# Sparse attention and a softplus feed-forward on one core: weight conversion begun later and its steps queued behind the attention's

## The chip, the cores and the metric

The kernel runs on one core of a Trainium2 chip. The metric is device time in microseconds (us); lower is better. The kernel before took 1484.01 us (median of three runs, 1479.19 to 1485.22).

The core's engines work from queues of their own, each in order: TensorE (PE; its weight loads are PEld) multiplies and transposes, VectorE (DVE) and ScalarE (ACT) work on tiles and read TensorE's results from PSUM, GpSimd (POOL) works on tiles in SBUF, and SyncE (SP) issues all transfers here.

## The reference

For each of 8 x 8 heads with 576 rows of 64, attention in which only scores within tau of the row's maximum count, then a feed-forward on the 4608 rows of 512:

```python
scores = scale * np.matmul(q, k.transpose(0, 1, 3, 2))
thresh = np.max(scores, axis=-1, keepdims=True) - tau
scores = np.where(scores >= thresh, scores, -1000000000.0)
attn = np.exp(scores - max); attn = attn / (sum(attn) + 1e-09)
x = (attn @ v), heads side by side                  # 4608 x 512
h = x @ w_in                                        # 512 x 2048
g = np.maximum(h, 0.0) + np.log1p(np.exp(-np.abs(h)))
out = g @ w_out                                     # 2048 x 512
```

q, k and v are float32, the two weight matrices are 64-bit floats.

## The kernel before, in words

**Attention.** A unit is a pair of heads of one batch: 32 units, each with nine tiles of 128 rows, so 288 tiles. TensorE works in a reduced float format, so every operand is split into a high part and a low part and each product is made from two or three. For a tile, `scores` (L375) puts 128 x 576 scores into one of two PSUM buffers of two banks, `row_max` (L395) reduces them on VectorE, `exps` (L405) writes the exponentials on ScalarE, `mask` (L409) zeroes on VectorE what lies below the threshold and adds up the row. Then `weights_T` (L428) transposes the masked tile on TensorE, `weights_hi` (L468, ScalarE) and `weights_lo` (L483) make the two parts, and for each of four groups of columns in a unit `values` (L509) multiplies with v into a PSUM bank. The two halves of that result are added by `values_out` (L522): ScalarE copies one half to SBUF (through `copy`, L462), VectorE adds the other. In the first 36 tiles (TG) the low parts are made by TensorE and ScalarE (L492, L494, L464), later by VectorE (L125).

**Feed-forward.** From tile 41 on, `hidden` (L597, L610 to L614), `softplus` (L625) and `project` (L659, L668 to L672) work through chunks of 512 rows, spread between the steps of the attention so that TensorE has work while a tile waits for the other engines.

**PSUM.** Four banks (tag "g", GB = 4) serve the transposes of q and k, the hidden units, the outputs, the sums of the values and the row scales; four more hold the scores.

**Weights.** Both matrices come in 32 blocks of 128 x 512 64-bit floats. `to_f32` (L134) loads one (L168, 512 KB) and turns the bit patterns into float32: ScalarE takes the absolute value of the high words (L176), GpSimd clamps (L177), VectorE shifts left (L181), puts in the sign (L182) and three bits of the low words (L184). `parts` then splits the result on GpSimd (L118, L125). A block of w_in goes back to DRAM in that form (L208), and its pieces of memory are free again; a block of w_out stays. There are NFC = 16 pieces (`free`, `held`): a block in conversion takes two where it can, and a w_out block keeps a further one. With too few pieces (`took` below 2) the block uses other buffers and all its steps are emitted at once behind the load (`later_` then calls at once); with none at all, `force` first carries out deferred work early until some come free.

**Order.** The program is emitted tile by tile along a string of letters, PAT0 for the first 36 tiles and PAT after that:

```python
PAT = "ThRlefmpfxSwp"
PAT0 = "RMTeShlfpfxwp"
```

R, e, m, S are the reduction, exponential and mask of the next tile and the scores of the one after it, M, T, h, l the mask, transposes and parts of the present one, f a piece of feed-forward, x the unit's extras (among them `values`), w the next weight block if its time has come (one every second tile, from tile 1 to tile 63). Each p is a *point*, two in a tile: `defer(n, f)` (L754) emits f at the n-th point from now. So WD = 2 defers the first step of a block by one tile behind its load. The order of emission is a priority and not yet the order in the queues: the framework works out, when the program is built, when each instruction would be ready, and puts into each engine's queue the first that is ready. An instruction that is emitted later can so be queued ahead of one whose inputs come later in that calculation. On the chip the queue is then kept in order. `tc.add_manual_dep(..., NoSync, ...)` forces an order of two instructions of one queue without a semaphore.

Of the kernel before, what the change touches and what calls it, by code (L numbers as in the profile page):

```python
# [9 lines left out]
F32 = mybir.dt.float32  # L10
F32R = mybir.dt.float32r
U32 = mybir.dt.uint32
AF = mybir.ActivationFunctionType
ALU = mybir.AluOpType
# [18 lines left out]
LAG0 = 5  # L33
PAT = "ThRlefmpfxSwp"
PAT0 = "RMTeShlfpfxwp"
WD = 2
ST = (1, 3, 4, 4, 5, 6, 6, 8)
VO = (1, 1, 1, 0)
RT = 1
# [19 lines left out]
def tile_kernel(ctx: ExitStack, tc: tile.TileContext, q, k, v, tau, w_in, w_out, out):  # L59
# [8 lines left out]
    nc = tc.nc  # L68
# [5 lines left out]
    HS = S // 2  # L74
# [3 lines left out]
    NFC = DFF // P  # L78
# [28 lines left out]
                            op0=ALU.is_ge, op1=ALU.mult)  # L107
# [8 lines left out]
    def hi_of(eng, out_, in_):  # L116
        if eng is nc.gpsimd:
            eng.tensor_scalar(out=out_, in0=in_, scalar1=1.0, scalar2=1.0, op0=ALU.mult, op1=ALU.mult)  # L118
        elif eng is nc.scalar:
            eng.copy(out_, in_)  # L120
        else:
            eng.tensor_copy(out_, in_)  # L122

    def lo_of(eng, out_, in_, hi):
        eng.tensor_tensor(out=out_, in0=in_, in1=hi.bitcast(F32), op=ALU.subtract)  # L125
# [2 lines left out]

    free, held = [NFC], [0]

    def piece(dt, name):
        return cpool.tile([P, 2, DM], dt, tag="wo", bufs=NFC, name=name)

    def to_f32(src, want, name, then):  # L134

        keep = 1 if want else 0
        while free[0] < 1 + keep and free[0] < NFC - held[0]:
            force()  # L140
        took = max(0, min(2, free[0] - keep))
        if took:
            words = piece(F32R, f"wc_{name}")
        else:
            words = wpool.tile([P, 2, DM], F32R, tag="wi", bufs=WB, name=f"wc_{name}")
        if took > 1:
            m = piece(F32, f"wa_{name}")[:, 0, :]
        else:
            m = fpool.tile([P, 512], F32, tag="st", bufs=NST, name=f"ws_{name}")
        free[0] -= took + keep  # L150
        held[0] += keep

        later_ = defer if took > 1 else lambda n, f: f()
        w = piece(F32R, f"wo_{name}") if want else words

        def done():
            free[0] += took

        def parts():
            hi_of(nc.gpsimd, w[:, 0, :], m)  # L160
            lo_of(nc.gpsimd, w[:, 1, :], m, w[:, 0, :])

        if src.dtype == F32:
            nc.sync.dma_start(m, src)
            later_(WD, lambda: then(parts, w, done))
            return
        words = words.bitcast(U32).rearrange("p a n -> p (a n)")
        nc.sync.dma_start(words, src.bitcast(U32))  # L168
        words = words.rearrange("p (n t) -> p n t", t=2)
        low, high = words[:, :, 0], words[:, :, 1]  # L170
        mu = m.bitcast(U32)

        def first():
            nc.scalar.activation(m, high.bitcast(F32), AF.Abs, scale=2.0 ** 16)  # L176
            nc.gpsimd.tensor_scalar(out=m, in0=m, scalar1=W_MAX, scalar2=W_MIN, op0=ALU.min, op1=ALU.max)  # L177
            later_(1, second)

        def second():  # L180
            nc.vector.tensor_scalar(out=mu, in0=mu, scalar1=3, scalar2=None, op0=ALU.logical_shift_left)  # L181
            nc.vector.scalar_tensor_tensor(out=mu, in0=high, scalar=0x80000000, in1=mu,  # L182
                                           op0=ALU.bitwise_and, op1=ALU.bitwise_or)
            nc.vector.scalar_tensor_tensor(out=mu, in0=low, scalar=29, in1=mu,  # L184
                                           op0=ALU.logical_shift_right, op1=ALU.bitwise_or)
            later_(1, lambda: then(parts, w, done))

        later_(WD, first)

    ready = set()  # L190
# [25 lines left out]
    def prep_w_out(fc):  # L216
        def split(parts, w, free):
            wo[fc] = w
            parts()
            free()  # L220
            ready.add(("o", fc))

        to_f32(w_out[fc * P:(fc + 1) * P, :], True, f"o{fc}", split)
# [25 lines left out]
    for b in range(B):  # L249
        for kind in (("one", "two") if b < NSPLIT else ("all",)):  # L250
            for hp in range(NPAIR):
                s = Unit()
# [118 lines left out]
    e_all = cpool.tile([P, 2, S], F32, name="e_all")  # L371
# [31 lines left out]
        s.m[t] = (negm, thr)  # L403

    def exps(s, t):  # L405
        nc.scalar.activation(e_all[:, s.half[t], :].rearrange("p (h n) -> p h n", h=2), s.sp[t][:, :, 0:HS],  # L406
                             AF.Exp, bias=s.m[t][0], scale=1.0)

    def mask(s, t):  # L409
        e2 = e_all[:, s.half[t], :].rearrange("p (h n) -> p h n", h=2)  # L410
        nc.vector.scalar_tensor_tensor(out=e2, in0=s.sp[t][:, :, 0:HS], scalar=s.m.pop(t)[1], in1=e2,  # L411
                                       op0=ALU.is_ge, op1=ALU.mult, accum_out=s.sums[:, s.tiles.index(t):s.tiles.index(t) + 1])

    def group(s, g):
        if g not in s.grp:
# [45 lines left out]

    def copy(s, out_, in_):  # L462
        if s.neg:
            nc.scalar.activation(out_, in_, AF.Copy, scale=-1.0)  # L464
        else:
            nc.scalar.copy(out_, in_)  # L466

    def weights_hi(s, t):  # L468
        main, rest = s.sp[t]
        for g, c0, s0, n in s.place[t]:  # L470
            copy(s, group(s, g)[0][:, 0:NC, c0:c0 + n], main[:, :, s0:s0 + n])
        both = rests(s, t)
        if len(both) == 2:

            (g, c0, _, n), = s.place[both[0][0]]
            copy(s, group(s, g)[0][:, NC, c0:c0 + 2 * n].rearrange("p (k n) -> p k n", k=2),
                 rest.unsqueeze(1).to_broadcast([P, 2, n]))
            return
        for x, rows, up, _ in both:
            for g, c0, s0, n in s.place[x]:  # L480
                copy(s, group(s, g)[0][up, NC, c0:c0 + n], rest[rows, s0:s0 + n])
# [27 lines left out]
    def values(s, g):  # L509
        if g == 0:  # L510
            s.xp = apool.tile([P, S], F32, tag="xp", name=f"xp_{s.i}")
        j, x0, n, _ = s.groups[g]
        h, l = s.grp[g]
        vt = s.vt[j]
        o = ps_g.tile([P, 512], F32, tag="g", name=f"pv_{s.i}_{g}")
        for c in range(NC):
            nc.tensor.matmul(o[:, 0:n], vt[:, c, :], h[:, c, 0:n], start=(c == 0), stop=False)  # L517
            nc.tensor.matmul(o[:, 0:n], vt[:, c, :], l[:, c, 0:n], start=False, stop=False)  # L518
        nc.tensor.matmul(o[:, 0:n], vt[:, NC, :], h[:, NC, 0:n], start=False, stop=True)
        defer(1, lambda: values_out(s, g, o))  # L520

    def values_out(s, g, o):  # L522
        j, x0, n, _ = s.groups[g]
        keep = slice(j * D, (j + 1) * D)
        move = slice((1 - j) * D, (2 - j) * D)
        xs = s.xp[keep, x0:x0 + n]
        copy(s, xs, o[move, 0:n])
        if s.neg:
            nc.vector.tensor_tensor(out=xs, in0=xs, in1=o[keep, 0:n], op=ALU.subtract)
        else:  # L530
            nc.vector.tensor_tensor(out=xs, in0=o[keep, 0:n], in1=xs, op=ALU.add)

    def row_scales(s):
        nt = len(s.tiles)
# [219 lines left out]
    def defer(n, f):  # L754
        if n == 0:
            f()
        else:
            later.append((now["p"] + n, f))
# [8 lines left out]
    def force():  # L767
        _, f = later.pop(0)
        f()
# [6 lines left out]
    while sum(u.T for u in chunks) < NT:  # L776
# [4 lines left out]
        b, o = divmod(u.t0 + u.T - 1, S)  # L781
# [20 lines left out]
    for kind, g in WL:  # L802
        for m in range(4):
            n = len(prep)
# [75 lines left out]
    scores(*tiles[0])  # L880
    row_max(*tiles[0])
    exps(*tiles[0])
    scores(*tiles[1])
    for j in range(2):
# [3 lines left out]
    done = 0.0  # L888
    for g, (cur, t) in enumerate(tiles):
# [5 lines left out]
        for step in PAT0 + ("m" if g == TG - 1 else "") if g < TG else PAT:  # L895
            if step == "T":
                weights_T(cur, t)
            elif step == "h":
                weights_hi(cur, t)
            elif step == "l":  # L900
                weights_lo(cur, t)
            elif step == "R" and nxt:
                row_max(*nxt)
            elif step == "e" and nxt:
                exps(*nxt)
            elif step == "m" and nxt:
                mask(*nxt)
            elif step == "M":
                mask(cur, t)
            elif step == "f":  # L910
                upto += quota / PAT.count("f")
                while done < upto:
                    done += next(ffn)
            elif step == "x":
                extras(cur.i, cur.tiles.index(t))
            elif step == "S" and g + 2 < NS:
                scores(*tiles[g + 2])
            elif step == "w":
                while prep and prep[0][0] <= g:
                    _, f, a = prep.pop(0)  # L920
                    f(*a)
            elif step == "p":
                point()
# [38 lines left out]
```

## Time and profile before

| | |
|---|---|
| median of three runs | 1484.01 us |
| profiled execution | 1484.28 us, span 1482.5 us, mean granted TensorE clock 0.984 |
| busy: TensorE, its weight loads | 1411.4 us (95%), 1198.7 us (81%) |
| busy: VectorE, ScalarE, GpSimd | 1008.7 us (68%), 873.1 us (59%), 600.4 us (40%) |
| moved by DMA | 189.95 MB |
| mask L411 | 288 times, 815 ns each |
| exponential L406 | 288 times, 750 ns each |
| copy and addition of a sum (L466, L531; 400 to 1200 us) | 81 times, 418 and 472 ns (medians) |

Times are counted from the first instruction. A row of a timeline has the start, the length, the engine, the line and the tiles it writes and reads (out<-in); in brackets stands how long the engine was idle before it, and what ended that. A row of waits has who waited for whom, the total in us, how often, and the longest. Matmuls overlap, so a busy TensorE isn't TensorE at its peak; the granted clock (PEclk, 1.00 or 9 is full) says at what speed it ran. The first step on the first weight block stands at 12.8 us and the last load of one at 287.8 us, so the conversion lies in the first 300 us.

### The profile page before, as it was taken

Reading aid. Unit: us, or ns where it says so; the run is one execution under the profiler, and the core shown is the slowest. Engines: PE = TensorE matmul, PEld = TensorE weight load, DVE = VectorE, ACT = ScalarE, POOL = GpSimd, SP = SyncE. Lnnn points to the kernel's source line nnn. Section 1 sums busy time; section 2 is a strip of 40 time slices with the busy share of each in tenths; the row PEclk is TensorE's granted clock in tenths of the full one; section 3 lists DMA queues with packets and bytes.
Section 4 is the critical chain, followed back from the end, with each engine's and each line's share of the span. In section 5 each row is a group of like instructions: output and inputs, shape, how many; then the busy total and the mean of one; then the engine's idle time right before and its main releaser. Section 6 shows DMA issues by size and latency. Waiting matters only on the chain.

```text
span 1482.5 us, 23938 instructions
## 1 busy us (share of the span) xinstructions
PE 1411.4 (95%) x8024; PEld 1198.7 (81%) x8024; DVE 1008.7 (68%) x2251; ACT 873.1 (59%) x1671; POOL 600.4 (40%) x629
## 2 busy tenths in 40 slices
PE   5887889999999999999999999999999999999998
PEld 4777668788888888888888888888888888788887
DVE  6878778777777777777777777777777777411111
ACT  5777677565766576666666676657665666411110
POOL 4657565534433443344333443334334331323221
PEclk9999899999999999999999999999999999999999
DMA  6756575434443454335334544345333532343321
GB/s 183 199 151 193 151 215 173 130 104 134 129 120 116 119 157 115 98 102 151 110 105 113 149 118 119 108 134 152 114 113 100 153 99 81 103 142 120 120 88 43
DMA packets 131210, 189.95 MB, mean 128 GB/s; under 512 B 35312, under 2 KB 86800, under 8 KB 131088
## 3 DMA queue, kind: packets, MB, share of 16 engines
q1 hardware_dynamic: 131088, 188.43, 44.4%
q8 instruction: 64, 1.05, 0.3%
q14 instruction: 58, 0.48, 0.1%
HBM read 140.51 MB, written 27.41 MB: 113 GB/s over the span
## 4 chain that ended last, share of the span: by engine, by line
PE 76%; DVE 7%; ACT 5%; DMA 4%; issue 3%; POOL 3%; SPq 1%; POOLq 0%; ACTq 0%; DVEq 0%
PE s L392 10%; PE h L612 8%; PE h L610 8%; PE h L614 8%; PE o L672 7%; PE o L670 7%; PE o L668 7%; PE s L444 7%; PE pv L518 4%; PE pv L517 4%; DMA wc_i<-in_moe_w_in_dram 2%; PE tr L333 2%; DVE e_all L411 1%; DVE negm L398 1%; POOL g L125 1%
## 5 line engine op out<-in xcount | busy, mean ns | idle before, releaser
L466 ACT CAST gH<-s 128x512 fp32r<-128x512 f32 (+1 forms) x448 | 186.7, 466 | 150.7 <-PE s L444 145.9
L125 POOL TENSOR_TENSOR g<-st,g 128x512 fp32r<-128x512 f32 x144 | 191.8, 1350 | 193.6 <-DVE g L122 184.2
L411 DVE SCALAR_TENSOR_TENSOR e_all<-s,thr,e_all 128x576 f32<-128x576 f32 x288 | 234.4, 815 | 38.0 <-ACT e_all L406 34.6
L398 DVE TENSOR_REDUCE negm<-s 128x1 f32<-128x576 f32 x288 | 217.2, 755 | 48.5 <-PE s L392 40.8
L672 PE MATMUL o<-wo_o,g 128*128 128x512 f32 x576 | 232.8, 404 | 5.3 <-POOL g L125 5.3
L668 PE MATMUL o<-wo_o,g 128*128 128x512 f32 x576 | 233.5, 405 | 0.5 <-ACT g L120 0.4
L612 PE MATMUL h<-xl,wi 128*128 128x512 f32 x576 | 233.1, 405 | 0.0
L610 PE MATMUL h<-xh,wi 128*128 128x512 f32 x576 | 230.5, 400 | 0.4 <-ACT kT L337 0.4
L614 PE MATMUL h<-xh,wi 128*128 128x512 f32 x576 | 230.4, 400 | 0.0
L670 PE MATMUL o<-wo_o,g 128*128 128x512 f32 x576 | 229.9, 399 | 0.0
L406 ACT ACTIVATE e_all<-s,negm 128x576 f32<-128x576 f32 x288 | 216.0, 750 | 12.4 <-DVE negm L398 6.9
L125 DVE TENSOR_TENSOR gL<-s,gH 128x512 fp32r<-128x512 f32 (+1 forms) x280 | 175.0, 634 | 48.1 <-ACT gH L466 44.2
L392 PE MATMUL s<-kT,qT 128*128 128x288 f32 x1024 | 194.2, 312 | 7.4 <-DVE gH L125 4.4
L392 PEld LDWEIGHTS s<-kT,qT 128*128 128x128 f32 x1024 | 151.1, 193 | 25.1 <-issue 14.3
L444 PE MATMUL s<-identr,e_all 128*128 128x128 f32 x1008 | 155.2, 277 | 4.8 <-DVE e_all L411 4.7
L122 DVE CAST g<-st 128x512 fp32r<-128x512 f32 x128 | 57.8, 489 | 149.8 <-ACT st L632 149.3
L518 PE MATMUL pv<-gL,vt 128*128 128x320 f32 (+1 forms) x512 | 145.4, 304 | 5.0 <-DVE gL L125 4.8
L632 ACT ACTIVATE st<-h 128x512 f32<-128x512 f32 x144 | 78.3, 596 | 117.7 <-PE h L614 117.1
L517 PE MATMUL pv<-gH,vt 128*128 128x320 f32 (+1 forms) x512 | 145.6, 303 | 1.3 <-ACT gH L466 1.3
L672 PEld LDWEIGHTS o<-wo_o,g 128*128 128x128 f32 x576 | 109.2, 190 | 29.5 <-POOL g L125 10.9
L444 PEld LDWEIGHTS s<-identr,e_all 128*128 128x128 f32 x1008 | 116.0, 141 | 21.0 <-DVE e_all L411 12.8
L610 PEld LDWEIGHTS h<-xh,wi 128*128 128x128 f32 x576 | 108.9, 189 | 23.1 <-ACT kT L337 0.7
(105 smaller groups left out, 2381.2 us busy)
## 6 DMA issues: line engine op xcount, KB each, us to landing
wi<-wi_d SPq DMA_DIRECT2D x144, 512.0 KB
qT<-qT SPq DMA_DIRECT2D x124, 128.0 KB
R<-r_d SPq DMA_DIRECT2D x64, 144.0 KB
kn<-in_k_dram SPq DMA_DIRECT2D x32, 256.0 KB
qn<-in_q_dram SPq DMA_DIRECT2D x32, 256.0 KB
vn<-in_v_dram SPq DMA_DIRECT2D x32, 256.0 KB
wc_i<-in_moe_w_in_dram SPq DMA_DIRECT2D x16, 512.0 KB
wi_d<-wc_i SPq DMA_DIRECT2D x32, 256.0 KB
```

The lines of the kernel that those rows point to most:

```text
L125: eng.tensor_tensor(out=out_, in0=in_, in1=hi.bitcast(F32), op=ALU.subtract)
L392: nc.tensor.matmul(sp[:, hf, 0:HS], lhs, s.kT[j][:, k0 + hf * HS:k0 + (hf + 1) * HS], start=(m == 0), stop=(m == len(parts) - 1))
L398: nc.vector.reduce_max(negm, s.sp[t][:, :, 0:HS], axis=AX.XY, negate=True)
L406: nc.scalar.activation(e_all[:, s.half[t], :].rearrange("p (h n) -> p h n", h=2), s.sp[t][:, :, 0:HS], AF.Exp, bias=s.m[t][0], scale=1.0)
L411: nc.vector.scalar_tensor_tensor(out=e2, in0=s.sp[t][:, :, 0:HS], scalar=s.m.pop(t)[1], in1=e2, op0=ALU.is_ge, op1=ALU.mult, accum_out=s.s ...
L444: nc.tensor.matmul(main[:, c, :], e[:, c0:c0 + P], ident, is_transpose=True, start=True, stop=True)
L610: nc.tensor.matmul(h, wi[:, 0, cc, :], u.h[cc], start=(cc == 0), stop=False)
L612: nc.tensor.matmul(h, wi[:, 0, cc, :], u.l[cc], start=False, stop=False)
L614: nc.tensor.matmul(h, wi[:, 1, cc, :], u.h[cc], start=False, stop=(cc == NCC - 1))
L668: nc.tensor.matmul(o, gh[:, sl], wo[fc][:, 0, :], start=(i == 0), stop=False)
L670: nc.tensor.matmul(o, gh[:, sl], wo[fc][:, 1, :], start=False, stop=False)
L672: nc.tensor.matmul(o, gl[:, sl], wo[fc][:, 0, :], start=False, stop=(i == QF - 1))
```

## The change

A helper `behind` forces an instruction into its queue behind the last exponential (`exped`) or mask (`masked`) that has been emitted. Converted blocks begin four points, two tiles, after their load. ScalarE's step stands behind an exponential; VectorE's three steps are emitted one at a time, two points apart while fewer than eight w_out blocks are held and one point apart later, and each stands behind a mask. Blocks with `took` below 2 are converted at once, as before. The copy of every values' sum stands behind an exponential, and its addition is deferred by a further point and stands behind a mask. Loads, arithmetic and GpSimd's instructions are the same.

```diff
-WD = 2
+WD = 4
...
+    masked, exped = [], []
+
+    def behind(i, others):
+        if others:
+            tc.add_manual_dep(i.ins, others[-1].ins.name, mybir.DependencyInfo(
+                mybir.DependencyClass.NoSync, mybir.DependencyReason.DATA), reason="order")
...
+        step = 2 if held[0] < NFC // 2 else 1
...
         def first():
-            nc.scalar.activation(m, high.bitcast(F32), AF.Abs, scale=2.0 ** 16)
+            i = nc.scalar.activation(m, high.bitcast(F32), AF.Abs, scale=2.0 ** 16)
+            if took > 1:
+                behind(i, exped)
             nc.gpsimd.tensor_scalar(out=m, in0=m, scalar1=W_MAX, scalar2=W_MIN, op0=ALU.min, op1=ALU.max)
-            later_(1, second)
-
-        def second():
-            nc.vector.tensor_scalar(...)                # L181
-            nc.vector.scalar_tensor_tensor(...)         # L182
-            nc.vector.scalar_tensor_tensor(...)         # L184
-            later_(1, lambda: then(parts, w, done))
+            later_(1, lambda: second(0))
+
+        def second(n):
+            if n == 0:
+                i = nc.vector.tensor_scalar(...)
+            elif n == 1:
+                i = nc.vector.scalar_tensor_tensor(...)
+            else:
+                i = nc.vector.scalar_tensor_tensor(...)
+            if took > 1:
+                behind(i, masked)
+            if n < 2:
+                later_(step, lambda: second(n + 1))
+            else:
+                later_(1, lambda: then(parts, w, done))
...
     def exps(s, t):
-        nc.scalar.activation(...)
+        exped.append(nc.scalar.activation(...))
...
     def mask(s, t):
-        nc.vector.scalar_tensor_tensor(...)
+        masked.append(nc.vector.scalar_tensor_tensor(...))
...
     def values_out(s, g, o):
-        copy(s, xs, o[move, 0:n])
-        if s.neg:
-            nc.vector.tensor_tensor(out=xs, in0=xs, in1=o[keep, 0:n], op=ALU.subtract)
-        else:
-            nc.vector.tensor_tensor(out=xs, in0=o[keep, 0:n], in1=xs, op=ALU.add)
+        behind(copy(s, xs, o[move, 0:n]), exped)
+
+        def add():
+            if s.neg:
+                i = nc.vector.tensor_tensor(out=xs, in0=xs, in1=o[keep, 0:n], op=ALU.subtract)
+            else:
+                i = nc.vector.tensor_tensor(out=xs, in0=o[keep, 0:n], in1=xs, op=ALU.add)
+            behind(i, masked)
+
+        defer(1, add)
```

More of the change, by code (lines that the diff above doesn't have):

```diff
@@ L175, in first @@
         def first():
-            nc.scalar.activation(m, high.bitcast(F32), AF.Abs, scale=2.0 ** 16)
+            i = nc.scalar.activation(m, high.bitcast(F32), AF.Abs, scale=2.0 ** 16)
+            if took > 1:
+                behind(i, exped)
             nc.gpsimd.tensor_scalar(out=m, in0=m, scalar1=W_MAX, scalar2=W_MIN, op0=ALU.min, op1=ALU.max)
-            later_(1, second)
-        def second():
[L181 to L185, printed above, removed]
-            later_(1, lambda: then(parts, w, done))
+            later_(1, lambda: second(0))
+        def second(n):
+            if n == 0:
+                i = nc.vector.tensor_scalar(out=mu, in0=mu, scalar1=3, scalar2=None, op0=ALU.logical_shift_left)
+            elif n == 1:
+                i = nc.vector.scalar_tensor_tensor(out=mu, in0=high, scalar=0x80000000, in1=mu,
+                                                   op0=ALU.bitwise_and, op1=ALU.bitwise_or)
+            else:
+                i = nc.vector.scalar_tensor_tensor(out=mu, in0=low, scalar=29, in1=mu,
+                                                   op0=ALU.logical_shift_right, op1=ALU.bitwise_or)
+            if took > 1:
[4 more added lines that the diff above has]
+                later_(1, lambda: then(parts, w, done))
         later_(WD, first)
@@ L405, in exps @@
     def exps(s, t):
-        nc.scalar.activation(e_all[:, s.half[t], :].rearrange("p (h n) -> p h n", h=2), s.sp[t][:, :, 0:HS],
-                             AF.Exp, bias=s.m[t][0], scale=1.0)
+        exped.append(nc.scalar.activation(e_all[:, s.half[t], :].rearrange("p (h n) -> p h n", h=2),
+                                          s.sp[t][:, :, 0:HS], AF.Exp, bias=s.m[t][0], scale=1.0))
     def mask(s, t):
         e2 = e_all[:, s.half[t], :].rearrange("p (h n) -> p h n", h=2)
-        nc.vector.scalar_tensor_tensor(out=e2, in0=s.sp[t][:, :, 0:HS], scalar=s.m.pop(t)[1], in1=e2,
-                                       op0=ALU.is_ge, op1=ALU.mult, accum_out=s.sums[:, s.tiles.index(t):s.tiles.index(t) + 1])
+        masked.append(nc.vector.scalar_tensor_tensor(
+            out=e2, in0=s.sp[t][:, :, 0:HS], scalar=s.m.pop(t)[1], in1=e2, op0=ALU.is_ge, op1=ALU.mult,
+            accum_out=s.sums[:, s.tiles.index(t):s.tiles.index(t) + 1]))
     def group(s, g):
@@ L463, in copy @@
         if s.neg:
-            nc.scalar.activation(out_, in_, AF.Copy, scale=-1.0)
-        else:
-            nc.scalar.copy(out_, in_)
+            return nc.scalar.activation(out_, in_, AF.Copy, scale=-1.0)
+        return nc.scalar.copy(out_, in_)
     def weights_hi(s, t):
@@ L526, in values_out @@
         xs = s.xp[keep, x0:x0 + n]
-        copy(s, xs, o[move, 0:n])
-        if s.neg:
-            nc.vector.tensor_tensor(out=xs, in0=xs, in1=o[keep, 0:n], op=ALU.subtract)
-        else:
-            nc.vector.tensor_tensor(out=xs, in0=o[keep, 0:n], in1=xs, op=ALU.add)
+        behind(copy(s, xs, o[move, 0:n]), exped)
[6 more added lines that the diff above has]
+        defer(1, add)
     def row_scales(s):
```

## The prediction, made before the changed kernel had run

> **What bounds the kernel now.** I read the page first, then a table of stretches, then TensorE's waits in the opening, then the instructions around single gaps. The page gives the span, and the clock that TensorE was granted in 40 slices of 37 us:
>
> ```profile
> span 1482.5 us, 23938 instructions
> ...
> PEclk9999899999999999999999999999999999999999
> ```
>
> The profiled execution took 1484.28 us, 1.8 more than its span; the median of the three runs is 1484.01, so a sum made against the one holds for the other. The table says where TensorE has time to give back (columns: stretch, length, then each engine's busy us; PEclk is the granted clock):
>
> ```profile
> 0.00:50.00 50.00, 31.95 (x198) 27.97 (x198) 37.02 (x70) 32.34 (x73) 29.22 (x41) 0.97 0.66 180
> 50.00:100.00 50.00, 40.42 (x263) 35.66 (x261) 38.70 (x78) 37.11 (x87) 27.12 (x32) 0.90 0.68 195
> 100.00:150.00 50.00, 40.14 (x277) 36.20 (x278) 42.67 (x86) 39.85 (x95) 32.69 (x37) 0.93 0.61 166
> 150.00:200.00 50.00, 40.81 (x215) 33.01 (x214) 36.14 (x79) 32.87 (x63) 27.72 (x32) 0.90 0.59 169
> 200.00:250.00 50.00, 45.71 (x262) 38.08 (x263) 42.73 (x92) 34.87 (x65) 29.73 (x33) 0.97 0.64 193
> 250.00:300.00 50.00, 46.33 (x259) 39.18 (x257) 38.66 (x88) 32.21 (x61) 29.52 (x33) 0.93 0.52 149
> 400.00:600.00 200.00, 198.06 (x1177) 170.66 (x1176) 150.85 (x349) 130.03 (x243) 75.56 (x79) 1.00 0.43 120
> ```
>
> From 400 on TensorE is busy 198.06 of 200 us at full clock: no order of the other engines can win more than 1% there. In the first 300 us, the stretch in which the 32 weight blocks are converted, it is busy 245.4, so 54.6 us are idle, and the clock falls short by 0.03, 0.10, 0.07, 0.10, 0.03 and 0.07 of 50 us each, 20 us more. Any large gain must come from these 75 us. What TensorE waits for in them (total, times, longest):
>
> ```profile
> PE tm L444 <- DVE e_all L411: 18.8, 13, 3.9
> PE tr L333 <- DVE k L125: 6.3, 1, 6.3
> PE tr L441 <- DVE e_all L411: 5.5, 7, 2.0
> PE pv L518 <- DVE gL L125: 4.8, 3, 3.4
> PE s L392 <- DVE gH L125: 3.5, 2, 3.3
> ```
>
> The 6.3 are the first load. Nearly all the rest ends with VectorE, the mask (L411) first: 54.6 - 6.3 = 48.3 us idle, and 20 / 48.3 = 0.41 us of lost clock for each of them.
>
> **Why the mask is late.** One gap, instruction by instruction (start, length, instruction, idle time before it):
>
> ```profile
> 86.09 1.50 DVE L181 TENSOR_SCALAR wa_o<-wa_o 128x512 uint32<-128x512 uint32 x1 [0.33 <-POOL wa_o L177]
> ...
> 86.97 0.74 ACT L406 ACTIVATE e_all<-s,negm 128x576 f32<-128x576 f32 x1
> ...
> 87.62 0.82 DVE L182 SCALAR_TENSOR_TENSOR wa_o<-wc_o,wa_o 128x512 uint32<-128x512 uint32 x1
> ...
> 88.94 0.79 DVE L184 SCALAR_TENSOR_TENSOR wa_o<-wc_o,wa_o 128x512 uint32<-128x512 uint32 x1
> ...
> 91.15 0.82 DVE L411 SCALAR_TENSOR_TENSOR e_all<-s,thr,e_all 128x576 f32<-128x576 f32 x1
> ...
> 92.12 1.09 PE L444 MATMUL tm<-identr,e_all 128*128 128x128 f32 x4 [2.88 <-DVE e_all L411]
> ```
>
> The exponential was there at 87.7, but the three steps of one weight block (with the addition of a values' sum between them) stood ahead of the mask, which began at 91.15: 3.4 us late, and TensorE lay 2.88. Two other forms of the same thing:
>
> ```profile
> 20.80 0.68 ACT L176 ACTIVATE wa_i<-wc_i 128x512 f32<-128x512 f32 x1 [2.53 <-DMA wc_i<-in_moe_w_in_dram]
> ...
> 23.31 0.50 PE L494 MATMUL tl<-gH,identr 128*128 128x512 f32 x1 [1.98 <-ACT gH L464]
> ...
> 265.89 0.43 DVE L181 TENSOR_SCALAR wa_o<-wa_o 128x512 uint32<-128x512 uint32 x1 [4.90 <-POOL wa_o L177]
> ...
> 266.71 0.63 PE L518 MATMUL pv<-gL,vt 128*128 128x320 f32 x1 [3.38 <-DVE gL L125]
> ```
>
> First ScalarE's queue stands on a weight load that hasn't landed, with attention behind it; then VectorE's queue stands on GpSimd's clamp for 4.9 us. In the whole opening these waits of the queue heads are:
>
> ```profile
> ACT wa_i L176 <- DMA wc_i<-in_moe_w_in_dram: 10.1, 8, 2.8
> ...
> DVE wa_o L181 <- POOL wa_o L177: 8.3, 5, 4.9
> ...
> DVE wa_i L181 <- POOL wa_i L177: 7.5, 5, 3.2
> ```
>
> **The change, part by part.** No arithmetic is added, so each step keeps its length:
>
> ```profile
> L176 ACT ACTIVATE wa_i<-wc_i x16: 664/682/692, 12.8 to 210.5; 128x512 f32<-128x512 f32 x16
> ...
> L181 DVE TENSOR_SCALAR wa_i<-wa_i x16: 410/428/1479, 17.1 to 213.4; 128x512 uint32<-128x512 uint32 x16
> L182 DVE SCALAR_TENSOR_TENSOR wa_i<-wc_i,wa_i x16: 629/692/1721, 19.3 to 216.4; 128x512 uint32<-128x512 uint32 x16
> L184 DVE SCALAR_TENSOR_TENSOR wa_i<-wc_i,wa_i x16: 682/716/1157, 22.6 to 219.5; 128x512 uint32<-128x512 uint32 x16
> ```
>
> *Begun two tiles later, ScalarE's step behind an exponential.* The load is issued where it was; its first reader comes a tile (3 to 4 us) later, and not before the exponential of that tile. The waits on the load go: 10.1 us of ScalarE. Behind the waiting step there now stands nothing urgent, since the exponential is ahead of it.
>
> *VectorE's three steps one by one, each behind a mask.* Per block 0.43 + 0.69 + 0.72 = 1.8 us of VectorE stay, but one step of 0.7 us stands between two masks, or two of different blocks, instead of three in a row. I went through the gaps of 0.5 us and more and took those in which a weight step (or the addition of a sum) stood ahead of the late mask or part, counting no more than its delay: thirteen, from 16.5 (1.1 of its 3.9 us) and 23.31 (all 1.98) to 92.12 (2.88) and 266.71 (3.38), together 24.3 us, half of the 48.3. Bounds: 0, if the same work on a VectorE that is busy 236 of these 300 us makes other masks late; 24.3, if it only fills idle time. I take half, 12 us, as L181 still follows GpSimd's clamp by only half a tile and can stand on it as before (8.3 + 7.5 us). With the clock at 0.41 per us that is 12 + 5 = 17 us of gain.
>
> That the clock follows the gaps is in the trace:
>
> ```profile
> 207.17 1.19 PE L392 MATMUL s<-kT,qT 128*128 128x288 f32 x4 [1.23 <-DVE gL L125]
> ...
> 209.13 0.63 PE L670 MATMUL o<-wo_o,g 128*128 128x512 f32 x1
> ...
> 212.78 0.39 PE L670 MATMUL o<-wo_o,g 128*128 128x512 f32 x1
> ```
>
> The same product takes 0.63 us two us after a gap of 1.23, and 0.39 five us after it. The Trainium skill ("TensorE: Matmul & The Clock Gate", the part on the clock gate) has the half clock set in after at least one idle window of about 3.4 us. By that rule gaps of 1 to 3 us would cost no clock, the 5 us fall away, and the sum would end at about 1477 (an estimate); the rows here disagree, so the sum keeps them.
>
> *The pieces of memory.* A block in conversion now keeps its two pieces for 8 to 13 points (half tiles) and not for 4 to 7, and 16 pieces serve these and the finished output weights. Counted from the code, block 28 finds too few and, like 30 and 31 before, is converted right behind its load, while 29 is pushed through early to free pieces for 30: three or four such blocks instead of the two seen here.
>
> ```profile
> L176 ACT ACTIVATE ws_o<-wc_o x2: 673/675/677, 284.5 to 291.2; 128x512 f32<-128x512 f32 x2
> ```
>
> Price: nothing if the work around hides it, as it did for these two, and at most a gap like that at 266.71 with its clock, 3.4 x 1.41 = 4.8 us. I take 2.4. The loads of blocks 16 to 27 find only the pieces just given back, so SyncE's queue can stand on them, with the swaps of the queries behind; I cost that at nothing, for the pieces are given back half a tile or more ahead, and it would be seen as those swaps landing late.
>
> *The sums of the values.* The copy is held behind an exponential that mostly ran ahead of it already. The addition comes half a tile later and behind a mask, for all 128 sums. In the first 36 tiles the mask in question is the present tile's and already done. Later it is that of the tile after next:
>
> ```profile
> 607.76 0.43 DVE L531 TENSOR_TENSOR xp<-pv,xp 64x256 f32<-64x256 f32 x1 [1.42 <-ACT xp L466]
> ...
> 611.06 0.82 DVE L411 SCALAR_TENSOR_TENSOR e_all<-s,thr,e_all 128x576 f32<-128x576 f32 x1
> ...
> 855.89 0.41 DVE L531 TENSOR_TENSOR xp<-pv,xp 64x256 f32<-64x256 f32 x1
> ```
>
> The addition moves from 607.8 to after 611.9, and the sum's PSUM bank is held 4.1 us longer. Gain: VectorE no longer stands on the copy (1.42 here), worth nothing while TensorE is at 99%. Cost: one bank of four held longer, four times in nine tiles; between 0 and the rival's price below. I take 2.
>
> Sum: 1484.28 - 17 + 2.4 + 2 = 1471.7, say 1472.
>
> **The rivals.** *The gaps only move* (0.20). VectorE is busy 236 of 300 us in the opening and does the same work in a stricter order; a reduction or a part now stands behind the steps that the mask has passed, and L181 still stands on the clamp. Then only ScalarE's waits on loads count: the gap at 23.31 and the share of that at 16.5, 3.1 us and 1.3 of clock, less the 2.4: 1482. The Trainium skill speaks for it ("SBUF — State Buffer", the part on its two separate sides): VectorE and GpSimd take a shared pair of ports by turns, each for a whole instruction. The trace agrees in L181's 1479 ns against a median of 428; steps that are moved meet GpSimd's as before. Also here belongs that the order hardly changes because the steps lay behind those masks already; against it stand the four rows from 86.09 on.
>
> *Slower: the PSUM banks run out* (0.15). From the 34 sums between the rows at 607.76 and 855.89 and their neighbours' products and last reads I worked out how many of the four banks for sums, hidden units, outputs and transposes are in use: all four in some 11% of that time, an estimate. If one in ten of the 112 sums beyond the first 36 tiles meets that, and TensorE waits half of the 4.1 us each time, this costs 11 x 2.05 = 23 us: 1472 + 23 = 1495. It decides from 6 such waits on (12.3 us eats the gain); ten make it slower by over 0.5%. For it: a bank is awaited in order by TensorE's queue. Against it: the order of the queues is worked out when the program is built and can put a transposition or scores ahead.
>
> *All of it goes* (0.10): all 24.3 us and their clock, 34 us: 1450.
>
> **How the numbers follow.** The forecast has 0.55 and its own range 1460 to 1480; 0.05 of it lies above 1476.6. About 0.5% (7.4 us) is what a measurement of this kernel can tell from no change, so faster is below 1476.6: 0.50 + 0.10 = 0.60; within: 0.05 + 0.20 = 0.25; slower, above 1491.4: 0.15. The range of 8 in 10 reaches from the case in which all goes to just short of the banks' price: 1450 to 1491.
>
> **What would show it.** Right: idle time of TensorE in the first 300 us down from 54.6 to about 43, clock there above 0.95 in most stretches; no wait of L176 on its load while blocks are deferred; the three steps of a block apart, each after a mask; the additions after the mask of the next tile but one, and 400 to 600 still at 198. Wrong: the opening's idle time unchanged with other instructions ahead of the masks; or TensorE below 196 of 200 us in the middle, with the additions as what ended its waits.

## The result, and the profile after

The changed kernel took 1492.23 us (median of six runs, 1489.92 to 1493.06), the kernel before in the same runs 1483.37: a ratio of 1.0068, 95% interval [1.0053, 1.0083]. It is slower by about 9 us, and the time lies just above the forecast's range. The profiled executions took 1492.60 and 1484.28 us. In the tables below a change is told against the kernel before timed with it on the same chip, whose median was 1480.6 to 1483.4; the profiled execution of before, 1484.28 us, lies 1 to 4 us above that.

The table of stretches of the kernel after, in the columns of the one shown of before:

```profile
0.00:50.00 50.00, 34.26 (x222) 30.55 (x222) 33.40 (x68) 34.36 (x78) 21.00 (x33) 1.00 0.53 144
50.00:100.00 50.00, 37.81 (x263) 33.54 (x263) 39.26 (x80) 36.96 (x90) 28.82 (x35) 0.93 0.66 184
100.00:150.00 50.00, 39.87 (x249) 36.21 (x249) 39.86 (x78) 36.92 (x86) 31.55 (x36) 0.83 0.62 176
150.00:200.00 50.00, 39.34 (x206) 32.41 (x206) 40.80 (x87) 31.59 (x62) 30.77 (x34) 0.86 0.64 189
200.00:250.00 50.00, 46.57 (x267) 38.66 (x268) 41.63 (x88) 34.95 (x65) 30.81 (x34) 1.00 0.67 200
250.00:300.00 50.00, 44.54 (x248) 35.77 (x247) 45.32 (x93) 34.30 (x64) 29.83 (x34) 0.97 0.45 138
...
400.00:600.00 200.00, 196.48 (x1163) 169.18 (x1162) 148.76 (x344) 130.33 (x241) 75.72 (x79) 1.00 0.42 120
```

TensorE is busy 242.4 of the first 300 us (245.4 before) and the clock lost 20.5 us (20): the opening, where all the gain was to come from, is level. And from 400 to 600 it is busy 196.48 us, not 198.06. To see where the two programs part, compare the time at which the same tile is masked. First of before, then of after, tile 99 and tile 270:

```profile
443.32 0.82 DVE L411 SCALAR_TENSOR_TENSOR e_all<-s,thr,e_all 128x576 f32<-128x576 f32 x1
...
1199.75 0.82 DVE L411 SCALAR_TENSOR_TENSOR e_all<-s,thr,e_all 128x576 f32<-128x576 f32 x1
```

```profile
443.49 0.82 DVE L431 SCALAR_TENSOR_TENSOR e_all<-s,thr,e_all 128x576 f32<-128x576 f32 x1
...
1206.59 0.82 DVE L431 SCALAR_TENSOR_TENSOR e_all<-s,thr,e_all 128x576 f32<-128x576 f32 x1 [0.50 <-ACT e_all L426]
```

At tile 99 the new kernel is 0.2 us behind, at tile 270 6.8 us: it loses 6.7 us over 171 tiles, evenly (1.9 at tile 144, 3.4 at 198, 5.3 at 234). I call this *the loss of the middle*. From tile 90 (1.3 ahead) to tile 287 (8.1 behind) it is 9.4. TensorE's waits there, 400 to 1200 us, first in the kernel before, then after:

```profile
PE o L672 <- POOL g L125: 3.9, 10, 0.5
PE s L444 <- DVE e_all L411: 3.4, 10, 0.3
```

```profile
PE o L697 <- POOL g L125: 8.2, 10, 1.4
PE tr L353 <- DVE acc L710: 6.2, 10, 0.9
```

Together 7.3 us before and 14.4 after: the 7.1 us between them are about the loss. The wait on masks is gone, the outputs' wait on GpSimd has grown by 4.3, and one is new: a transposition of q waits for an addition of the *outputs*, with which it has nothing in common but the bank that it is to be written to. One such place, of before:

```profile
629.04 0.31 PE L519 MATMUL pv<-gH,vt 128*128 128x320 f32 x1
...
633.55 0.50 PE L333 MATMUL tr<-identr,q 128*128 128x128 f32 x4
```

```profile
631.24 0.47 DVE L531 TENSOR_TENSOR xp<-pv,xp 64x320 f32<-64x320 f32 x1
```

and the same place after:

```profile
631.14 0.31 PE L539 MATMUL pv<-gH,vt 128*128 128x320 f32 x1
...
636.41 0.51 PE L353 MATMUL tr<-identr,q 128*128 128x128 f32 x4 [0.60 <-DVE acc L710]
```

```profile
635.57 0.69 DVE L710 TENSOR_TENSOR acc<-o,acc 128x512 f32<-128x512 f32 x1
...
636.18 0.81 DVE L431 SCALAR_TENSOR_TENSOR e_all<-s,thr,e_all 128x576 f32<-128x576 f32 x1
...
636.91 0.48 DVE L553 TENSOR_TENSOR xp<-pv,xp 64x320 f32<-64x320 f32 x1
```

Before, the sum's bank was free at 631.7, ahead of the transposition at 633.55. After, the sum ends 2.1 us later like everything else, but its bank is free only at 637.4, after the mask, so the transposition waits for the next bank to come free, that of an output. From the last product of a sum to the end of its addition it is 1.19 us before and 5.41 us after (means over 26 sums between 600 and 860 us, worked out from the timelines). The transposition waits like this at two places in every 36 tiles (four units), some 0.6 us each time.

The outputs' wait has another form. At one place in every 36 tiles it is 1.37 us and not 0.50, because GpSimd's queue has another order there. Before, GpSimd goes straight to the low parts of the hidden units (g):

```profile
661.62 2.63 POOL L125 TENSOR_TENSOR g<-st,g 128x512 fp32r<-128x512 f32 x2 [2.50 <-DVE g L122]
```

After, a part of the feed-forward's input (xl) stands ahead of them:

```profile
663.58 1.38 POOL L125 TENSOR_TENSOR xl<-xst,xh 128x512 fp32r<-128x512 f32 x1 [2.59 <-ACT xh L120]
664.92 2.50 POOL L125 TENSOR_TENSOR g<-st,g 128x512 fp32r<-128x512 f32 x2
```

So part of the loss is an order that the framework worked out anew when the program was built. TensorE's queue shows the same between tiles 99 and 270: its order there differs from that of before, while in weights_only (below) it doesn't.

In the opening the forecast's mechanism was made, and did little. ScalarE's waits on weight loads are gone, as forecast (10.1 us on the w_in blocks before). VectorE's on the clamp are not:

```profile
DVE wa_i L194 <- POOL wa_i L188: 12.7, 10, 2.6
DVE wa_o L194 <- POOL wa_o L188: 3.2, 4, 1.9
```

15.9 us, against 15.8 before.

### The profile page after: what moved, and what is told of

Its sections match the earlier page's. It is cut to its first block, busy times and chain, and to the rows that moved or that the text cites. A ratio compares the mean times of both kernels' runs of the same rounds, so it can differ in the third digit from the quotient of the medians.

```text
span 1490.8 us, 23934 instructions
## 1 busy us (share of the span) xinstructions
PE 1410.2 (95%) x8024; PEld 1199.1 (80%) x8024; DVE 1012.3 (68%) x2251; ACT 876.5 (59%) x1671; POOL 600.2 (40%) x629
## 4 chain that ended last, share of the span: by engine, by line
PE 74%; DVE 9%; ACT 5%; POOL 4%; issue 3%; DMA 3%; SPq 1%; POOLq 0%; DVEq 0%; ACTq 0%
PE s L412 10%; PE h L635 8%; PE h L637 8%; PE h L639 8%; PE o L697 7%; PE o L695 7%; PE o L693 7%; PE s L465 6%; PE pv L537 4%; PE pv L538 3%; PE tr L353 2%; DVE negm L418 2%; DVE e_all L431 2%; ACT st L657 1%; ACT gH L486 1%
```

## The experiments

| kernel | what | median, us | ratio to before | loss of the middle, us |
|---|---|---|---|---|
| after | all of the change | 1492.23 | 1.0068 [1.0053, 1.0083] | 6.7 |
| weights_only | the weights' part | 1479.75 | 0.9990 [0.9978, 1.0002] | 0.0 |
| sums_only | the sums' part | 1487.98 | 1.0048 [1.0030, 1.0067] | 8.0 |
| add_not_deferred | after, addition one point sooner | 1482.10 | 1.0001 [0.9991, 1.0012] | 0.0 |
| bank_held | weights_only, and a late read of the bank | 1499.94 | 1.0120 [1.0100, 1.0140] | 9.0 |
| bank_not_held | the same late read from elsewhere | 1485.59 | 1.0025 [1.0009, 1.0040] | 1.1 |
| three_buffers | after, three softplus buffers | 1492.18 | 1.0069 [1.0042, 1.0096] | 6.7 |
| bank_freed_early | that, bank emptied early, addition late | 1487.36 | 1.0036 [1.0018, 1.0054] | -0.4 |
| sums_two_late | after, addition two points on | 1491.00 | 1.0069 [1.0057, 1.0082] | 9.6 |
| sums_three_late | after, addition three points on | 1482.54 | 1.0010 [0.9995, 1.0025] | 6.8 |
| late_sums_opening | sums_only in the first 72 tiles | 1481.61 | 1.0003 [0.9994, 1.0013] | 0.3 |
| both_opening | after, late sums in the first 72 tiles | 1482.09 | 1.0004 [0.9995, 1.0014] | 0.1 |
| shift_later | weights_only, VectorE's first step later | 1471.04 | 0.9932 [0.9917, 0.9947] | 0.1 |
| shift_three | that, one point more | 1478.39 | 0.9975 [0.9964, 0.9987] | 0.7 |
| shift_no_behind | shift_later, no forced places | 1475.42 | 0.9956 [0.9944, 0.9969] | 0.0 |
| before_shift | before, VectorE's steps later | 1477.36 | 0.9971 [0.9958, 0.9984] | 0.1 |

The last column is the difference to the kernel before in the time from the mask of tile 99 to that of tile 270, from one profiled execution of each. Three of these contain stretches in which TensorE was granted half its clock between these tiles. That lost clock is part of the column: 1.7 us in sums_only, 3.4 in sums_two_late and 5.1 in sums_three_late; the others lost none there.

**Which part.** *weights_only* leaves `values_out` as before; *sums_only* has the loads and `to_f32` of before and the new `values_out`.

> The new kernel with the sums added as before. Theory A (the late addition holds a PSUM bank of the four; the weights' part by itself gains a little): 1476 to 1482 us, the middle (400 to 1200 us) back at 198 of 200 us busy, and in the first 300 us none of TensorE's waits on the addition of a sum (six of 1.0 to 1.5 us in the new kernel). Theory B (the weights' new order costs the 8 us): 1490 or more.

> The kernel before with the late sums alone. Theory A: 1492 to 1498 us, middle at 195 to 197 of 200 us busy. Theory B: 1483, as before.

Measured: 1479.75 and 1487.98. The stretch from 400 to 600 us, of weights_only and then of sums_only:

```profile
400.00:600.00 200.00, 198.01 (x1173) 170.46 (x1172) 151.10 (x348) 129.81 (x242) 76.71 (x80) 1.00 0.43 119
```

```profile
400.00:600.00 200.00, 196.31 (x1163) 169.25 (x1162) 149.06 (x344) 129.18 (x239) 75.57 (x79) 1.00 0.42 119
```

The loss is the sums' alone. The weights' part gives nothing that can be told from no change. Two details of the expectations failed: sums_only came out 4 us below theory A's range, and in weights_only three of TensorE's waits of 1.0 to 1.5 us on the addition of a sum are left in the first 300 us.

**The bank, or the addition's place?** The late addition does two things: it holds a bank and it stands elsewhere in VectorE's queue. *bank_held* adds as before and then has VectorE read one column of the sum's bank (0.15 us) where the late addition would stand:

```diff
+        def last_read():
+            behind(nc.vector.tensor_copy(junk, o[:, 0:1]), masked)
+        defer(1, last_read)
```

> The weights' part as in the new kernel, the sums added as before, and a one-column read of the sum's bank by VectorE behind the mask where the addition would stand, so that only the bank is held late. Theory A (the bank): as the new kernel, 1488 to 1495 us, transpositions of q and k waiting in the middle. Theory C (the addition's place in VectorE's and ScalarE's queues, not the bank): as weights_only, within 2 us.

Measured: 1499.94, above the range expected, and 9.0 us lost in the middle. The addition ends 1.19 us after the sum, as in the kernel before, the late read 5.10 us after it. TensorE's waits from 400 to 1200 us:

```profile
PE o L698 <- POOL g L125: 5.0, 10, 0.7
PE tr L353 <- DVE acc L711: 3.5, 10, 0.4
```

The same wait of a transposition on an output's bank is there. These waits do not add up to the loss, though: between tiles 99 and 270 TensorE is idle only 3.8 us more than before, and counted busy 5.2 us more, mostly in transpositions and scores, whose order in its queue has changed too. How the held bank makes that part was not taken apart. Part of the 1499.94 is lost in the opening too (5.6 us behind at tile 90), where this read holds banks as well. *bank_not_held* reads the column from the identity matrix in SBUF, at the same place:

```diff
-            behind(nc.vector.tensor_copy(junk, o[:, 0:1]), masked)
+            behind(nc.vector.tensor_copy(junk, identr.bitcast(F32)[:, 0:1]), masked)
```

> bank_held with its late one-column read made from SBUF and not from the sum's bank: the same extra instruction of VectorE at the same place, no bank held. Bank theory: as weights_only, 1478 to 1483, nothing lost between tiles 99 and 270. If the extra instruction behind the mask was what cost: 1495 to 1500, some 9 us lost there.

Measured: 1485.59, above the range expected, but 1.1 us lost in the middle. Its waits there:

```profile
PE o L698 <- POOL g L125: 3.9, 10, 0.5
PE s L466 <- DVE e_all L432: 2.0, 6, 0.3
PE s L466 <- DVE junk L555: 2.0, 5, 0.6
```

No transposition waits, and TensorE's queue there has the order of before. With the bank held the instruction costs 9.0 us, without it 1.1.

The other way round: *bank_freed_early* keeps the addition behind its mask and has ScalarE copy the second half out as well. It takes the room for the copy from the softplus's buffers; *three_buffers* is the new kernel with those buffers.

```diff
-NST = 4
+NST = 3
...
+        ys = apool.tile([P, 320], F32, tag="ys", bufs=1, name=f"ys_{s.i}_{g}")[keep, 0:n]
+        nc.scalar.copy(ys, o[keep, 0:n])
...
-                i = nc.vector.tensor_tensor(out=xs, in0=o[keep, 0:n], in1=xs, op=ALU.add)
+                i = nc.vector.tensor_tensor(out=xs, in0=ys, in1=xs, op=ALU.add)
```

> The new kernel with both halves of a sum copied out of PSUM by ScalarE (128 more copies of 0.4 us), so that the addition stays behind its mask but the bank is free before it; the room for the copy is taken from the softplus's buffers (three instead of four). Looked at from tile 99 to tile 270, where the new kernel loses 6.6 us. Bank theory: below 2 us lost there against three_buffers' 6 or more. If the addition's place in VectorE's queue or the changed order is the cause: 5 us or more, as in three_buffers.

> The new kernel with three softplus buffers and nothing else, beside which bank_freed_early is read: 6 to 10 us lost between tiles 99 and 270 by every theory, more if the buffers matter too.

Measured: three_buffers loses 6.7 us in the middle, like the new kernel, and bank_freed_early gains 0.4, with the addition as late as there. Neither the transposition's wait nor GpSimd's other order is left there. So the loss of the middle hangs on the bank's late release, shown from both sides. What the runs do not separate is how much of it is a wait on the chip and how much the order that the framework works out once a bank is held longer. (bank_freed_early is 5.4 us behind at tile 90; with 128 more copies on ScalarE in the opening that can be, but it wasn't separated.)

**How late is too late.** *add_not_deferred* calls `add()` at once, still with `behind(i, masked)`, so it lies behind the mask of the next tile; *sums_two_late* and *sums_three_late* have `defer(2, add)` and `defer(3, add)`.

> The new kernel with the addition emitted with its copy, behind the last mask emitted by then (that of the next tile, not of the one after it). Theory A: the bank is given back some 4 us sooner, and most of the middle's loss goes: 1478 to 1484 us. Theory C: half of the loss stays, 1486 to 1490.

> The new kernel with the addition two points behind its copy in place of one, so that the bank is held for another half tile or more. Bank theory: the loss in the middle grows, 6.6 us to 12 or more, and the whole to 1498 to 1510. If only the addition's being behind a mask costs: as the new kernel, 1490 to 1494.

> The new kernel with the addition three points behind its copy. Two points left it behind the same mask as one (5.4 us from the sum's last product to the end of the addition in both traces); three put it behind the next mask, some 9.5 us. Bank theory: the loss between tiles 99 and 270, 6.6 us in the new kernel, at least doubles, and the whole comes to 1500 or more. If one late read costs the same however late: 1490 to 1494.

Measured: add_not_deferred has 1.19 us from the sum to its addition, and nothing lost: that mask was ahead of the addition already. sums_two_late has 5.41 us, as the new kernel: the last mask emitted by then is the same one, so this was not the dose that I meant it to be, and the time stayed. sums_three_late has up to 10.3 us (median 7.9), and both halves of the expectation failed: the whole takes as long as the kernel before. Its profile still shows 6.8 us lost in the middle, but of another kind. In that kernel the transposition's wait is gone and only one of the two is left:

```profile
PE o L697 <- POOL g L125: 8.2, 10, 1.4
```

That is 0.9 us more than all listed waits of before. Most of the 6.8 is lost clock, in three places, of which this is the first (the granted clock is the third figure from the end):

```profile
660.00:670.00 10.00, 8.81 (x44) 7.44 (x45) 4.98 (x12) 4.89 (x10) 4.94 (x6) 0.83 0.51 128
```

From 980 to 990 and from 1140 to 1150 us it is 0.83 as well, and three times 0.17 of 10 us is 5.1 us. This profiled execution, 1486.84 us, is also 4.3 above the median of its twelve runs. In the same way sums_two_late's 9.6 is 6.2 without its lost clock, with TensorE's instructions in the same order as in the new kernel. So a longer hold did not cost more; but with the order changed once more, sums_three_late is no clean test of how the loss grows with the hold, and why its opening is better than the new kernel's isn't settled.

**The opening.** *late_sums_opening* and *both_opening* make the sums late for units 0 to 7 alone:

```diff
-        defer(1, add)
+        defer(1 if s.i < 8 else 0, add)
```

> The kernel before with the late sums in the first eight units (72 tiles) alone. The profile of sums_only reached tile 90 8.7 us sooner than the one of before and lost 10.6 from there on. If the gain of the opening is real and the loss is the bank's, 1473 to 1477, faster than both kernels. If the opening's gain is chance of the profiled executions, 1480 to 1482.

> The new kernel with the late sums in the first eight units alone. Bank theory: the middle back at 198 of 200 us and 1480 to 1484, as the new kernel's profile is level with that of before at tile 90. If the loss is in the opening after all: 1488 or more.

Measured: 1.0003 and 1.0004. Late sums give nothing in the opening, and without them in the middle the new kernel is level with the one before. sums_only's lead of 8.7 us at tile 90 was for the most part chance: in sums_only and late_sums_opening the queues of all four computing engines have the same instructions in the same order for the first 72 tiles, and yet the two were 2.8 and 0.6 us ahead at tile 30, and 7.8 and 2.3 at tile 72. The granted clock would account for it: the one lost 10 us of clock in the first 300, the other 16.5.

So the question is why the weights' part gives so little. In weights_only VectorE still stands on the clamp:

```profile
DVE wa_i L194 <- POOL wa_i L188: 12.5, 10, 2.5
DVE wa_o L194 <- POOL wa_o L188: 5.9, 4, 2.7
```

18.4 us, more than before, and here is what that does to a mask:

```profile
52.91 0.43 DVE L194 TENSOR_SCALAR wa_i<-wa_i 128x512 uint32<-128x512 uint32 x1 [2.54 <-POOL wa_i L188]
53.37 0.42 DVE L549 TENSOR_TENSOR xp<-xp,pv 64x256 f32<-64x256 f32 x1
53.82 1.32 DVE L196 SCALAR_TENSOR_TENSOR wa_i<-wc_i,wa_i 128x512 uint32<-128x512 uint32 x1
55.17 0.76 DVE L418 TENSOR_REDUCE negm<-s 128x1 f32<-128x576 f32 x1
55.96 0.59 DVE L524 SCALAR_TENSOR_TENSOR gH<-tr,gH 64x128 fp32r<-64x128 f32 x2
56.57 0.82 DVE L431 SCALAR_TENSOR_TENSOR e_all<-s,thr,e_all 128x576 f32<-128x576 f32 x1
```

```profile
57.54 1.09 PE L465 MATMUL tm<-identr,e_all 128*128 128x128 f32 x4 [3.42 <-DVE e_all L431]
```

Behind the mask at 49.6 the first step waits 2.54 us for the clamp; then come a sum and the same block's second step (L196), although that was emitted a tile later, and the next mask and TensorE are late. Being behind one mask doesn't keep a step from standing ahead of the next. *shift_later* gives the clamp a second half tile:

```diff
-            later_(1, lambda: second(0))
+            later_(2, lambda: second(0))
```

> weights_only with VectorE's first step two points behind ScalarE's in place of one, so that GpSimd's clamp is done before it. If the opening's gain is eaten by VectorE standing on the clamp (12.7 us in ten waits in the new kernel's trace) ahead of masks: 1473 to 1477. If the steps only displace other work of a busy VectorE: 1479 to 1482.

Measured: 1471.04, ratio 0.9932 [0.9917, 0.9947], faster than both kernels. VectorE's waits on the clamp of the same blocks, then TensorE's first wait in the first 300 us:

```profile
DVE wa_i L194 <- POOL wa_i L188: 4.5, 6, 1.8
DVE wa_o L194 <- POOL wa_o L188: 4.5, 3, 2.6
```

```profile
PE tm L465 <- DVE e_all L431: 10.7, 8, 3.3
```

18.4 us have become 9.0 (and 2.3 on blocks converted at once), and the wait on the masks, 18.8 us before and 16.1 in weights_only, is 10.7. But most of the gain shows as clock. The first 300 us of weights_only and of shift_later:

```profile
0.00:300.00 300.00, 245.43 (x1481) 210.68 (x1482) 237.50 (x492) 210.20 (x442) 175.97 (x206) 0.94 0.61 176
0.00:300.00 300.00, 248.47 (x1542) 210.13 (x1543) 246.45 (x510) 217.84 (x459) 185.87 (x210) 0.97 0.62 180
```

TensorE is idle 3.0 us less, and loses some 10 us less to the clock (18.5 and 8.5, added up from stretches of 50 us). That is not one lucky profile: the mean granted clock was 0.984 to 0.988 in all eleven runs of weights_only and 0.992 to 0.994 in all six of shift_later, and half a percent of 1470 us is most of the 8.7 us between their medians. So the extra half tile is shown to bring the gain; that it does so through the clamp's waits and the masks is argued from these rows, and accounts for the smaller part of it directly.

*shift_three* has `later_(3, ...)`, *shift_no_behind* leaves out both `behind` calls of `to_f32`, *before_shift* is the kernel before with `later_(2, second)`.

> shift_later with three points in place of two between ScalarE's and VectorE's first step. If VectorE's remaining wait on the clamp (11.3 us in the first 300) still costs: 1466 to 1470. If the room is enough at two: 1470 to 1474; the pieces of memory are held half a tile longer, which may cost a few us.

> shift_later without the forced places behind exponentials and masks. If these places are needed for the gain: 1478 to 1484. If the two tiles behind the load and the spreading do it alone: 1470 to 1474.

> The kernel before with VectorE's steps on a weight block two points behind ScalarE's in place of one, nothing else. If room between the clamp and VectorE's first step is all that the gain of shift_later needs: 1470 to 1474. If the steps are still queued as soon as they are ready in the framework's calculation, deferral alone moves little: 1478 to 1483.

Measured: 0.9975, 0.9956 and 0.9971. shift_three, 1478.39, lies outside both of its ranges; before_shift and shift_no_behind fall between their two expectations: the room alone gives 4 to 5 us, two tiles and the spreading with it 6 to 7, and with the forced places 10. The steps share in it, and the room is what the change lacked: without it the other parts gave 1.4 us within noise. (In shift_no_behind TensorE's wait on masks is 20.6 us, more than before, and the kernel is faster all the same: that wait alone doesn't tell the time.) A third point is worse than two; ScalarE stands on loads again there, of blocks that found no pieces:

```profile
ACT ws_o L185 <- DMA wc_o<-in_moe_w_out_dram: 5.5, 3, 4.2
```

## Why the prediction was wrong, point by point

- *What bounds the kernel* held: no more than 1% to be won from 400 us on, and the opening's idle time ends with VectorE's masks.
- *ScalarE's step behind an exponential*: its waits on loads went, as said, and with them the gap at 23.31; the new kernel was 5.9 us ahead at tile 6. By tile 18 it was 0.7.
- *VectorE's three steps*: "I take half, 12 us", and with the clock 17, is the first step that failed. weights_only gives 1.4 us (0.9990 [0.9978, 1.0002]). The sentence that L181 "can stand on it as before (8.3 + 7.5 us)" was right to 0.1 us in the new kernel, and I priced it by halving a sum instead of taking out the gaps that such a wait makes. The rival "the gaps only move" was nearer (1482), and shift_later bears out its reason, that VectorE still stands on the clamp: with a half tile more for the clamp 10 us come.
- *The clock*: 20.5 us were lost for 57.6 idle, 20 for 54.6 before; without the 6.3 of the first load that is 0.40 and 0.41 for each idle us, as priced. But that is no fixed price: weights_only lost 18.5 for 54.6, shift_later 8.5 for 51.5 and sums_only 10 for 56.1. The prediction went by the rows of before against the rule of a whole idle window in the Trainium skill ("TensorE: Matmul & The Clock Gate", the part on the clock gate). In sums_three_late, too, half clock came about 2 us behind a gap of 1.37 us, so the rows still speak against that rule; what sets the amount the runs don't show.
- *The pieces of memory*: 2.4 us for more blocks converted at once. There were three, as counted. The waits of those steps in the new kernel are 1.0 us; the term wasn't measured by itself.
- *The sums of the values*: "I take 2" is the second step that failed, in size. The mechanism was the rival's, with its place (the bank, 4.1 us longer; measured 4.2), and its sign. Its price was 23 us, from one in ten sums meeting four banks in use; measured are 6.7 us between tiles 99 and 270, and 9.4 from tile 90 to tile 287, at fixed places in every 36 tiles rather than at random. "The order can put a transposition ahead" was half right: the order was worked out anew, but the transpositions of q still waited, and GpSimd's new order made the outputs wait longer, which the sum had no term for.
- *The sign*: two terms of 17 and -4.4 were really 1.4 (weights_only) and some -7 (sums_only) to -12 (the new kernel against weights_only). Half of the new kernel's loss would have left it at no change; with the gain as priced even this loss would have left it level or faster, so the chance of 0.15 for slower was too low mainly because the gain was too high.

## What to carry to other kernels

Forcing an instruction behind the urgent one moves its wait to the next urgent one unless what it waits for is given time as well: look at what the moved instruction's own inputs are late by. A last reader that is put off holds its PSUM bank until then; where the banks are few, count who asks for one in between, above all for work that the late instruction has nothing to do with, and compare the order of every queue, since a program whose banks come free later may be ordered anew. Before a loss in one profile is explained, take out what the granted clock cost in it.

## What the runs showed of the hardware

The same instructions in the same order in all four queues reached tile 30 2.2 us apart and tile 72 5.5 us apart in two profiled executions (sums_only and late_sums_opening), so a difference of that size in the opening between two single profiles proves nothing; the loss of the middle came out alike in the new kernel and in three_buffers, 6.7 us both times, neither with lost clock there.

The granted clock went to one half for 3.4 us behind TensorE gaps of 1.37 us at three of the five places of that gap in sums_three_late, and at none of the five in the new kernel. In the first 300 us, traces with 51.5 to 57.6 us of idle TensorE lost anything from 8.5 to 20.5 us of clock.

VectorE's weight steps still stretched in places after the change: in weights_only L196 took 1.32 us at 53.82, with GpSimd at work on a part of v, against a median of 0.69 for the same step before.
